# One core's bulk loads moved from SyncE's DMA queue to GpSimd's, with the large SBUF tensor at a multiple of 256 bytes

## The chip, the cores and the metric

The kernel runs on one core of a Trainium2 chip. The metric is the device time of one execution in microseconds (us). The time before is the median of 3 runs. A run and its profile are two things: the profile is one execution recorded by the hardware profiler, and its span runs from the first to the last instruction.

## The reference

One decode step of two branches that are mixed by a scalar gate: attention of one query against a cache of 65,536 keys and values in 32 heads, and a small gated feed-forward network. Everything is bfloat16.

```python
# x (1,1,512); k_cache, v_cache (1,32,65536,128); wq (512,4096); wo (4096,512)
# w_gate, w_up (512,1792); w_down (1792,512); gate_w (512)
g = sigmoid((x * gate_w).sum(-1))
q = (x @ wq)                                   # 32 heads of 128
scores = einsum(q, k_cache) * 128 ** -0.5      # 32 x 65536
p = softmax(scores)
a = einsum(p, v_cache) @ wo
b = (silu(x @ w_gate) * (x @ w_up)) @ w_down
return g * a + (1 - g) * b
```

The caches are 2 x 537 MB and each byte of them is used once, so nearly all of the 1,088 MB that the kernel reads are keys and values.

## The kernel before

A head's keys are 16.8 MB and are loaded in two halves, z = 0 and z = 1, of 8.4 MB; its values likewise. One such load is one DMA: 128 partitions, each a contiguous row of 64 KiB in HBM and in SBUF. All of them go into one large SBUF tensor, `mem` (128 partitions x 188,416 bytes), in which a place is counted in KiB: `KA`, `KZ` and `V0` are places for key halves, `VA` and `VZ` for value halves. The places overlap, so a load may start only when what lay there has been used.

What is done with a half: VectorE transposes keys in 8 pieces of 128 x 2048 four-byte words into `kt` (line 322 for head 0, lines 415 and 422 for later heads; each piece counts `ktdone` up by one), TensorE makes the scores from `kt` (line 472, `qkdone`), then the maximum, the exponential on ScalarE and a re-ordering of the probabilities on VectorE (line 331, 16 short copies for each half) follow, and TensorE multiplies the probabilities with the values straight from `mem` (line 525, 40 and 24 matmuls to a half, `pvdone`). A head's values are worked on while the next head's keys are being scored.

SyncE issues nearly all DMAs, in the order in which it is written, and waits ahead of each until the place is free. Its order: the four weights `wq`, `wg`, `wu`, `wd` (line 213); the first key half of head 0 as two DMAs of half the columns, `ka0` and `ka` (line 228); then, when the query is there (`s_q`), the second key half of head 0; when the 8 pieces of the first half are transposed (`ktdone` = 8), the first key half of head 1; when 13 are, the first value half of head 0; and so on. From head 1 the loop is key half 0 of the head after, value half 0, key half 1, value half 1, each behind one wait (lines 241 to 249):

```python
sp.wait_ge(s_q, 1)
load("k", 0, 1)
sp.wait_ge(ktdone, NP)          # NP = 8
load("k", 1, 0)
...
sp.wait_ge(pvdone, i * 4 + 7)
load("v", i + 1, 0)
```

The last value half is cut into 8 DMAs of falling size (line 258), and `wo` comes ahead of them, so that little work is left when the last bytes land. ScalarE issues the two 1 KB loads of `x` and `gate_w` at the start and half of the output; SyncE issues the other half of it. GpSimd has only four small memsets of constants at the start.

`mem` is allocated behind 16,384 bytes of reserved space and a few small constants, at byte 16,512 of each partition, which is 128 past a multiple of 256. All places in `mem` are multiples of 1,024 bytes from there.

Of the kernel before, what the change touches and what calls it, by code (L numbers as in the profile page):

```python
# [5 lines left out]
P = 128  # L6
KB = 512
# [5 lines left out]
BF16 = mybir.dt.bfloat16  # L13
# [8 lines left out]
def bass_gated_mix__mha_block_cached__swiglu_ffn__decode_kernel(  # L22
# [11 lines left out]
    out: bass.AP,  # L34
):
    _, H, S, Dh = A_k_cache.shape
    D = A_wq.shape[0]
    F = B_w_gate.shape[1]
# [3 lines left out]
    HR = R // 2  # L42
    NP = HR // PR
# [5 lines left out]
    KA, KZ, VA, VZ, V0 = 32, 0, 120, 96, 96  # L49
    MEM = 184  # L50
# [12 lines left out]
    WOJ, WO31 = V0, V0 + 1  # L63

    with ExitStack() as ctx:
        def sb(name, shape, dt):
            return ctx.enter_context(nc.sbuf_tensor(name, shape, dt))

        def psum(name, shape, dt):
            return ctx.enter_context(nc.psum_tensor(name, shape, dt))  # L70
# [1 line left out]
        def sem(name):  # L72
            return ctx.enter_context(nc.semaphore(name))
# [7 lines left out]
        psW = psum("psW", [P, 512], F32)  # L81
        psZ = psum("psZ", [P, 512], F32)

        mem = sb("mem", [P, MEM * KB], BF16)
        kt = sb("kt", [P, 2, 2 * PR * 32], U32)
        qd = sb("qd", [P, H, 4, 4], BF16)
        qcur = sb("qcur", [P, 4, 4], BF16)
        pa = sb("pa", [P, 512], BF16)
# [18 lines left out]
        fin = sb("fin", [P, 128], BF16)  # L107

        def at(kb, n):
            return mem[:, kb * KB:kb * KB + n]  # L110
# [7 lines left out]
        mrow, amx, Lt = psM[0:1, 0:128], psM[:, 256:257], psM[:, 257:258]  # L118
        gm = sc[0:1, 5:6]

        names = ("x", "gw", "wq", "wg", "wu", "wd", "ka0", "ka", "kz", "va", "vz", "wo", "wj", "w31")
        d = {n: sem("d_" + n) for n in names}
        dt_ = [sem(f"d_t{i}") for i in range(len(tail))]
        s_ones = sem("s_ones")
# [15 lines left out]
        s_q = sem("s_q")  # L140
# [7 lines left out]
        s_b = sem("s_b")  # L148
        s_dch = sem("s_dch")
        ktdone = sem("ktdone")  # L150
        qkdone = sem("qkdone")
        pvdone = sem("pvdone")
# [22 lines left out]
        s_fin = sem("s_fin")  # L175
        s_zz = sem("s_zz")
        s_out2 = sem("s_out2")
# [3 lines left out]
        out_dram = out.rearrange("a b (c n) -> (a b c) n", c=4)  # L181
        gw_dram = gate_w.rearrange("(a d) -> a d", a=1)
        w_dram = {
            "wq": A_wq.rearrange("(p c) n -> p (c n)", c=Dc),
            "wg": B_w_gate.rearrange("(p c) f -> p (c f)", c=Dc),
            "wu": B_w_up.rearrange("(p c) f -> p (c f)", c=Dc),
            "wd": B_w_down.rearrange("(p c) n -> p (c n)", c=FC),
            "wo": A_wo.rearrange("(p j) n -> p (j n)", p=P),
        }
        wj_dram = w_dram["wo"][:, 31 * D:32 * D]  # L190
        w31_dram = A_wo.rearrange("(h d) n -> h d n", d=Dh)[H - 1]
        WQ, WG, WU, WD, WO = V0, 0, 14, V0 + 64, 64
# [8 lines left out]
        def place(kind, h, z):  # L201
            if kind == "k":
                return (KA, V0)[z] if isinstance(h, int) and h == 0 else (KA, KZ)[z]
            return (VA, VZ)[z]

        def kv_dram(cache, h):
            if isinstance(h, int):
                return cache[0, h].rearrange("(b p r) d -> b p (r d)", b=2, p=P)
            return cache[0, ds(h, 1)].rearrange("a (b p r) d -> b (a p) (r d)", b=2, p=P)

        for n, kb in (("wq", WQ), ("wg", WG), ("wu", WU), ("wd", WD)):
            src = w_dram[n]
# [4 lines left out]
        ctx.callback(lambda: nc.sync.wait_ge(s_out2, 16))  # L217
        block = ctx.enter_context(nc.Block())

        @block.sync  # L220
        def _(sp):
            def load(kind, h, z):
                cache = A_k_cache if kind == "k" else A_v_cache
                sp.dma_start(at(place(kind, h, z), HR * Dh), kv_dram(cache, h)[z]).then_inc(d[kind + "az"[z]], 16)  # L224

            half = HR // 2 * Dh
            for n in range(2):
                sp.dma_start(at(KA + 32 * n, half), kv_dram(A_k_cache, 0)[0][:, n * half:n * half + half]).then_inc(
                    (d["ka0"], d["ka"])[n], 16)
            sp.wait_ge(s_q, 1)  # L230
            load("k", 0, 1)
            sp.wait_ge(ktdone, NP)
            load("k", 1, 0)
            sp.wait_ge(ktdone, 2 * NP - 3)
            sp.wait_ge(s_b, 1)
            load("v", 0, 0)
            sp.wait_ge(ktdone, 2 * NP + NP // 2)
            load("k", 1, 1)
            sp.wait_ge(pvdone, 5)
            load("v", 0, 1)  # L240
            with nc.sync.Fori(0, H - 2) as i:
                sp.wait_ge(ktdone, i * (2 * NP) + (4 * NP - 4))
                load("k", i + 2, 0)
                sp.wait_ge(pvdone, i * 4 + 7)
                load("v", i + 1, 0)
                sp.wait_ge(ktdone, i * (2 * NP) + (4 * NP + NP // 2))
                load("k", i + 2, 1)
                sp.wait_ge(pvdone, i * 4 + 9)
                load("v", i + 1, 1)
            sp.wait_ge(ktdone, 2 * NP * H - NP)  # L250
            sp.dma_start(at(WO, 31 * D), w_dram["wo"][:, 0:31 * D]).then_inc(d["wo"], 16)
            src = A_v_cache[0, H - 1].rearrange("(b p r) d -> b p (r d)", b=2, p=P)
            need = {0: (ktdone, 2 * NP * H - 4), 1: (ktdone, 2 * NP * H), 2: (pvdone, 4 * H - 1)}
            for n, (kb, r0, nr) in enumerate(tail):
                if n in need:
                    sp.wait_ge(*need[n])
                b, o = divmod(r0, HR)
                sp.dma_start(at(kb, nr * Dh), src[b][:, o * Dh:(o + nr) * Dh]).then_inc(dt_[n], 16)  # L258
            sp.wait_ge(pvdone, 4 * H)
            sp.dma_start(at(WOJ, D), wj_dram).then_inc(d["wj"], 16)  # L260
            sp.dma_start(at(WO31, D), w31_dram).then_inc(d["w31"], 16)
            sp.wait_ge(s_fin, 1)
            sp.dma_start(out_dram[2:4, :], fin[32:34, :]).then_inc(s_out2, 16)

        @block.scalar
        def _(act):
# [38 lines left out]
        def _(dve):  # L305
# [7 lines left out]
            def transposes(z):  # L313
                dve.wait_ge(d[("ka0", "kz")[z]], 16)
                for c, u in enumerate(k_order[z]):
                    i = NP * z + c
                    if i == NP // 2:
                        dve.wait_ge(d["ka"], 16)
                    if i >= 2:
                        dve.wait_ge(qkdone, i - 1)  # L320
                    src = at(place("k", 0, z) + 8 * u, PR * Dh).bitcast(U32)
                    nc.vector.transpose(kt[:, i % 2, :].rearrange("p (j r t) -> p r j t", j=2, t=32),  # L322
                                        src.rearrange("p (r j t) -> p r j t", j=2, t=32)).then_inc(ktdone, 1)

            def shuffle(z, s):
                c0 = 256 * z
                for g in range(4):
                    for b in range(4):
                        dst = pb[32 * g:32 * g + 32, c0:c0 + 256].rearrange("p (n b) -> p n b", b=4)[:, :, b]
                        sr = pa[32 * b:32 * b + 32, c0:c0 + 256].rearrange("p (n g) -> p n g", g=4)[:, :, g]  # L330
                        last = nc.vector.tensor_copy(dst, sr)  # L331
                last.then_inc(s, 1)
# [7 lines left out]
            def late(pv, sl, so):  # L340
                dve.wait_ge(pvdone, pv)
                shuffle(1, s_pbz)
                dve.wait_ge(s_L, sl)
                dve.wait_ge(s_or, so)
                nc.vector.reciprocal(Li, Lt).then_inc(s_li, 1)
# [57 lines left out]
            with nc.vector.Fori(1, H) as i:  # L403
                n = i * (2 * NP)
                v = i * 4
                dma = i * 16
                dve.wait_ge(d["ka"], dma + 16)
                for c, u in enumerate(k_order[0]):
                    if c == NP // 2:
                        dve.wait_ge(expdone, i)  # L410
                        dve.wait_ge(pvdone, v - 2)
                        shuffle(0, s_pba)
                    dve.wait_ge(qkdone, n + (c - 1))
                    src = at(KA + 8 * u, PR * Dh).bitcast(U32)
                    nc.vector.transpose(kt[:, c % 2, :].rearrange("p (j r t) -> p r j t", j=2, t=32),  # L415
                                        src.rearrange("p (r j t) -> p r j t", j=2, t=32)).then_inc(ktdone, 1)
                late(v, i, i)
                dve.wait_ge(d["kz"], dma + 16)
                for c, u in enumerate(k_order[1]):
                    dve.wait_ge(qkdone, n + (NP + c - 1))  # L420
                    src = at(KZ + 8 * u, PR * Dh).bitcast(U32)
                    nc.vector.transpose(kt[:, c % 2, :].rearrange("p (j r t) -> p r j t", j=2, t=32),  # L422
                                        src.rearrange("p (r j t) -> p r j t", j=2, t=32)).then_inc(ktdone, 1)
                top(i, n + 2 * NP)
# [206 lines left out]
```

## Time and profile before

| | |
|---|---|
| time, median of 3 runs | 2518.53 us (2518.48 to 2519.13) |
| profiled execution, first to last instruction (span) | 2517.0 us |
| busy: TensorE, VectorE, ScalarE, GpSimd | 68%, 56%, 3%, 0% |
| bytes read from HBM | 1087.77 MB, 432 GB/s over the span |
| SyncE's DMA queue (q1), share of the 16 DMA engines' span | 99.9% |

The profiled execution's own time is known only as its span. It is 1.5 us below the median of the runs, which also count what lies around the first and last instruction. In the views, "SPq" is SyncE's queue of instructions, "PEld" TensorE's weight load, and "to landing" the time from the issue of a DMA to its last semaphore increment. A wait is written as the engine and line that waited, and after an arrow what ended the wait.

### The profile page before, as it was taken

To read this page: it belongs to the slowest core of one execution; us is meant where nothing else is said; L and a number is where in the kernel's file an instruction comes from. 1 tells how busy PE (TensorE), PEld (TensorE's weight loads), DVE (VectorE), ACT (ScalarE), POOL (GpSimd) and SP (SyncE) were. 2 spreads that over 40 slices of the span, in tenths; PEclk is the share of its full clock that TensorE was granted. 3 is DMA by queue.
4 is the path that set the end of the run, shared out by engine and by line. 5 is a ranking of instruction groups with operands and counts; after the bars stand their busy time and mean duration, and the time that the engine had idled before them with its cause. 6 is when DMAs were issued, how large, how long until landed. Compare 5 with 4: busy or idle time off the path is not lost.

```text
span 2517.0 us, 51694 instructions
## 1 busy us (share of the span) xinstructions
PE 1710.9 (68%) x21624; PEld 979.2 (39%) x21624; DVE 1411.7 (56%) x1683; ACT 64.6 (3%) x195; POOL 0.2 (0%) x4
## 2 busy tenths in 40 slices
PE   4667756667667677676776766766767767667677
PEld 3334433333433334333443333343334433334334
DVE  4764565554655645646456555465564564645653
ACT  0000000000000000000000000000000000000000
POOL 0000000000000000000000000000000000000000
PEclk8577767677677676776776767767767767677677
DMA  9999999999999999999999999999999999999999
GB/s 419 435 433 433 433 433 433 433 434 433 434 433 433 433 433 433 433 433 433 433 433 433 433 433 434 435 433 434 434 433 433 434 434 433 433 433 433 434 433 395
DMA packets 20471, 1087.93 MB, mean 432 GB/s; under 512 B 2283, under 2 KB 2669, under 8 KB 2925
## 3 DMA queue, kind: packets, MB, share of 16 engines
q1 hardware_dynamic: 20452, 1087.78, 99.9%
q8 instruction: 9, 0.15, 0.0%
q14 instruction: 2, 0.01, 0.0%
q10 hardware_dynamic: 8, 0.00, 0.0%
HBM read 1087.77 MB, written 0.00 MB: 432 GB/s over the span
## 4 chain that ended last, share of the span: by engine, by line
DMA 71%; PE 27%; DVE 1%; issue 1%; SPq 0%; ACT 0%; DVEq 0%
DMA mem<-in_A_v_cache_dram 68%; PE psO L525 27%; DMA mem<-in_A_k_cache_dram 2%; DVE kt L322 1%; DMA mem<-in_A_wq_dram 0%; DVE kt L415 0%; SPq L224 0%; PE psM L456 0%; DVE pb L331 0%; PE psS L472 0%; SPq L258 0%; PE psZ L600 0%; DVE sm L336 0%; PE psW L561 0%; PE psM L547 0%
## 5 line engine op out<-in xcount | busy, mean ns | idle before, releaser
L472 PE MATMUL psS<-qcur,kt 128*128 128x4 bf16 x16384 | 573.0, 169 | 728.7 <-DVE kt L415 413.2
L525 PE MATMUL psO<-mem,pb 128*4 128x512 bf16 x3968 | 1042.3, 429 | 34.5 <-DMA mem<-in_A_v_cache_dram 34.1
L472 PEld LDWEIGHTS psS<-qcur,kt 128*128 128x128 bf16 x16384 | 534.0, 105 | 792.1 <-issue 789.7
L422 DVE STREAM_TRANSPOSE kt<-mem 128x2048 uint32<-128x2048 uint32 x248 | 547.6, 2275 | 405.9 <-DMA mem<-in_A_k_cache_dram 405.9
L415 DVE STREAM_TRANSPOSE kt<-mem 128x2048 uint32<-128x2048 uint32 x248 | 551.3, 2280 | 239.3 <-DMA mem<-in_A_k_cache_dram 238.3
L525 PEld LDWEIGHTS psO<-mem,pb 128*4 128x4 bf16 x3968 | 359.8, 93 | 660.4 <-issue 241.3
L331 DVE COPY pb<-pa 32x64 bf16<-32x64 bf16 x1024 | 233.5, 228 | 15.1 <-ACT pa L288 1.5
L338 DVE TENSOR_REDUCE sc<-psM 1x1 f32<-1x128 f32 x32 | 8.9, 279 | 334.9 <-PE psM L547 334.9
L336 DVE TENSOR_REDUCE sm<-psS 128x1 f32<-128x512 f32 x32 | 22.1, 692 | 42.2 <-PE psS L472 42.2
L322 DVE STREAM_TRANSPOSE kt<-mem 128x2048 uint32<-128x2048 uint32 x16 | 35.4, 2277 | 16.9 <-DMA mem<-in_A_k_cache_dram 16.9
L286 ACT ACTIVATE sm<-psM 128x1 f32<-128x1 f32 x32 | 5.5, 171 | 1223.4 <-PE psM L549 1223.4
L282 ACT ACTIVATE oTn<-psT,gcol 128x1 f32 (+1 forms) x31 | 8.2, 264 | 1036.8 <-PE psT L499 1036.8
L499 PE MATMUL psT<-ident,orow 4*128 4x1 f32 x256 | 33.5, 248 | 0.5 <-ACT orow L280 0.5
L499 PEld LDWEIGHTS psT<-ident,orow 4*128 4x128 f32 x256 | 30.8, 186 | 1.2 <-ACT orow L280 0.6
L280 ACT ACTIVATE orow<-psO,sm 4x512 f32<-4x512 f32 x31 | 21.0, 678 | 130.3 <-PE psO L525 126.0
L288 ACT ACTIVATE pa<-psS,sm 128x512 bf16<-128x512 f32 x32 | 22.0, 687 | 1.0
L549 PE MATMUL psM<-sc,onesf 1*128 1x1 f32 x64 | 12.3, 259 | 11.9 <-DVE sc L338 11.9
L561 PE MATMUL psW<-pb,mem 128*128 128x1 bf16 x512 | 14.6, 165 | 6.5 <-DMA mem<-in_A_v_cache_dram 6.0
L549 PEld LDWEIGHTS psM<-sc,onesf 1*128 1x128 f32 x64 | 9.6, 186 | 21.5 <-DVE sc L338 21.5
L561 PEld LDWEIGHTS psW<-pb,mem 128*128 128x128 bf16 x512 | 14.1, 102 | 7.6 <-issue 5.5
L553 PEld LDWEIGHTS psM<-sm,onesf 128*128 128x128 f32 x64 | 9.7, 191 | 14.7 <-issue 13.5
L553 PE MATMUL psM<-sm,onesf 128*128 128x1 f32 x64 | 12.4, 264 | 1.1 <-ACT pa L288 1.1
(72 smaller groups left out, 93.1 us busy)
## 6 DMA issues: line engine op xcount, KB each, us to landing
mem<-in_A_v_cache_dram SPq DMA_DIRECT2D x3, 4096.0 KB, 29.4
mem<-in_A_k_cache_dram SPq DMA_DIRECT2D x2, 4096.0 KB, 38.9
mem<-in_A_wq_dram SPq DMA_DIRECT2D x1, 4096.0 KB, 12.3
mem<-in_A_wo_dram SPq DMA_DIRECT2D x1, 3968.0 KB, 36.6
mem<-in_A_v_cache_dram SPq DMA_DIRECT2D x1, 2048.0 KB, 32.9
mem<-in_B_w_gate_dram SPq DMA_DIRECT2D x1, 1792.0 KB, 16.1
mem<-in_B_w_up_dram SPq DMA_DIRECT2D x1, 1792.0 KB, 21.4
mem<-in_B_w_down_dram SPq DMA_DIRECT2D x1, 1792.0 KB, 25.2
```

Source lines behind the costliest of these rows:

```text
L288: nc.scalar.activation(pa[:], psS[:], ACT.Exp, bias=nbias, scale=SCALE, accum_out=rsum).then_inc(expdone, 1)
L322: nc.vector.transpose(kt[:, i % 2, :].rearrange("p (j r t) -> p r j t", j=2, t=32), src.rearrange("p (r j t) -> p r j t", j=2, t=32)).then ...
L331: last = nc.vector.tensor_copy(dst, sr)
L336: nc.vector.reduce_max(mxs, psS[:], AX_X).then_inc(s_mx, 1)
L415: nc.vector.transpose(kt[:, c % 2, :].rearrange("p (j r t) -> p r j t", j=2, t=32), src.rearrange("p (r j t) -> p r j t", j=2, t=32)).then ...
L422: nc.vector.transpose(kt[:, c % 2, :].rearrange("p (j r t) -> p r j t", j=2, t=32), src.rearrange("p (r j t) -> p r j t", j=2, t=32)).then ...
L472: last = nc.tensor.matmul(psS[:, o:o + 4] if j is None else psS[:, ds(j * (2 * PR) + o, 4)], ktb[b][:, je // 2, r, :, je % 2], qcur[:, je, ...
L499: last = nc.tensor.matmul(psT[:, 0:1], orow[0:4, i * Dh:(i + 1) * Dh], ident[0:4, i:i + 1], start=(i == 0), stop=(i == 3))
L525: last = nc.tensor.matmul(psO[0:4, :], pb[:, k_col[256 * z + r]:k_col[256 * z + r] + 4], vt[:, r * Dh:(r + 4) * Dh], start=(z == 0 and par ...
L549: nc.tensor.matmul(amx, onesf[0:1, :], gm, start=True, stop=True).then_inc(s_ar, 1)
L553: nc.tensor.matmul(Lt, onesf[:], rsum, start=True, stop=True).then_inc(s_L, 1)
L561: last = nc.tensor.matmul(psW[:, 0:1], vt[:, r * Dh:(r + 1) * Dh], pb[:, col:col + 1], start=(r0 + r == 0), stop=(r0 + r == R - 1))
```

## The change

All DMAs behind `ka0` and `ka` are written in a program of GpSimd's, with the same waits in the same order; SyncE keeps the four weights, the first key half of head 0 and its half of the output. The second piece of that first key half has a semaphore of its own, `ka1`, since the later key halves count theirs from another queue. `mem` is placed at a multiple of 256 bytes: it moves from byte 16,512 to byte 16,640 of each partition. The instructions of TensorE, VectorE and ScalarE stay as they are and in their order; GpSimd gets 136 DMAs and their waits.

```diff
-        def sb(name, shape, dt):
-            return ctx.enter_context(nc.sbuf_tensor(name, shape, dt))
+        def sb(name, shape, dt, align=32):
+            return ctx.enter_context(nc.sbuf_tensor(name, shape, dt, align_bytes=align))
...
-        mem = sb("mem", [P, MEM * KB], BF16)
+        mem = sb("mem", [P, MEM * KB], BF16, 256)
...
         @block.sync
         def _(sp):
+            for n in range(2):
+                sp.dma_start(at(KA + 32 * n, half), kv_dram(A_k_cache, 0)[0][:, n * half:n * half + half]).then_inc(
+                    (d["ka0"], d["ka1"])[n], 16)
+            sp.wait_ge(s_fin, 1)
+            sp.dma_start(out_dram[2:4, :], fin[32:34, :]).then_inc(s_out2, 16)
+
+        @block.gpsimd
+        def _(pool):
             def load(kind, h, z):
                 cache = A_k_cache if kind == "k" else A_v_cache
-                sp.dma_start(at(place(kind, h, z), HR * Dh), kv_dram(cache, h)[z]).then_inc(d[kind + "az"[z]], 16)
-
-            half = HR // 2 * Dh
-            for n in range(2):
-                sp.dma_start(at(KA + 32 * n, half), kv_dram(A_k_cache, 0)[0][:, n * half:n * half + half]).then_inc(
-                    (d["ka0"], d["ka"])[n], 16)
-            sp.wait_ge(s_q, 1)
+                pool.dma_start(at(place(kind, h, z), HR * Dh), kv_dram(cache, h)[z]).then_inc(d[kind + "az"[z]], 16)
+
+            pool.wait_ge(s_q, 1)
             load("k", 0, 1)
-            sp.wait_ge(ktdone, NP)
+            pool.wait_ge(ktdone, NP)
             load("k", 1, 0)
...
-            with nc.sync.Fori(0, H - 2) as i:
-                sp.wait_ge(ktdone, i * (2 * NP) + (4 * NP - 4))
+            with nc.gpsimd.Fori(0, H - 2) as i:
+                pool.wait_ge(ktdone, i * (2 * NP) + (4 * NP - 4))
                 load("k", i + 2, 0)
...
                     if i == NP // 2:
-                        dve.wait_ge(d["ka"], 16)
+                        dve.wait_ge(d["ka1"], 16)
...
-                dve.wait_ge(d["ka"], dma + 16)
+                dve.wait_ge(d["ka"], dma)
```

More of the change, by code (lines that the diff above doesn't have):

```diff
@@ L119, in bass_gated_mix__mha_block_cached__swiglu_ffn__decode_kernel @@
         gm = sc[0:1, 5:6]
-        names = ("x", "gw", "wq", "wg", "wu", "wd", "ka0", "ka", "kz", "va", "vz", "wo", "wj", "w31")
+        names = ("x", "gw", "wq", "wg", "wu", "wd", "ka0", "ka1", "ka", "kz", "va", "vz", "wo", "wj", "w31")
         d = {n: sem("d_" + n) for n in names}
@@ L218, in bass_gated_mix__mha_block_cached__swiglu_ffn__decode_kernel @@
         block = ctx.enter_context(nc.Block())
+        half = HR // 2 * Dh
         @block.sync
         def _(sp):
+            for n in range(2):
[5 more added lines that the diff above has]
+        def _(pool):
             def load(kind, h, z):
@@ L231, in _ @@
+            pool.wait_ge(s_q, 1)
             load("k", 0, 1)
-            sp.wait_ge(ktdone, NP)
+            pool.wait_ge(ktdone, NP)
             load("k", 1, 0)
-            sp.wait_ge(ktdone, 2 * NP - 3)
-            sp.wait_ge(s_b, 1)
+            pool.wait_ge(ktdone, 2 * NP - 3)
+            pool.wait_ge(s_b, 1)
             load("v", 0, 0)
-            sp.wait_ge(ktdone, 2 * NP + NP // 2)
+            pool.wait_ge(ktdone, 2 * NP + NP // 2)
             load("k", 1, 1)
-            sp.wait_ge(pvdone, 5)
+            pool.wait_ge(pvdone, 5)
@@ L240, in _ @@
             load("v", 0, 1)
-            with nc.sync.Fori(0, H - 2) as i:
-                sp.wait_ge(ktdone, i * (2 * NP) + (4 * NP - 4))
+            with nc.gpsimd.Fori(0, H - 2) as i:
+                pool.wait_ge(ktdone, i * (2 * NP) + (4 * NP - 4))
                 load("k", i + 2, 0)
-                sp.wait_ge(pvdone, i * 4 + 7)
+                pool.wait_ge(pvdone, i * 4 + 7)
                 load("v", i + 1, 0)
-                sp.wait_ge(ktdone, i * (2 * NP) + (4 * NP + NP // 2))
+                pool.wait_ge(ktdone, i * (2 * NP) + (4 * NP + NP // 2))
@@ L247, in _ @@
                 load("k", i + 2, 1)
-                sp.wait_ge(pvdone, i * 4 + 9)
+                pool.wait_ge(pvdone, i * 4 + 9)
                 load("v", i + 1, 1)
-            sp.wait_ge(ktdone, 2 * NP * H - NP)
-            sp.dma_start(at(WO, 31 * D), w_dram["wo"][:, 0:31 * D]).then_inc(d["wo"], 16)
+            pool.wait_ge(ktdone, 2 * NP * H - NP)
+            pool.dma_start(at(WO, 31 * D), w_dram["wo"][:, 0:31 * D]).then_inc(d["wo"], 16)
             src = A_v_cache[0, H - 1].rearrange("(b p r) d -> b p (r d)", b=2, p=P)
@@ L255, in _ @@
                 if n in need:
-                    sp.wait_ge(*need[n])
+                    pool.wait_ge(*need[n])
                 b, o = divmod(r0, HR)
[L258 to L263, printed above, removed]
+                pool.dma_start(at(kb, nr * Dh), src[b][:, o * Dh:(o + nr) * Dh]).then_inc(dt_[n], 16)
+            pool.wait_ge(pvdone, 4 * H)
+            pool.dma_start(at(WOJ, D), wj_dram).then_inc(d["wj"], 16)
+            pool.dma_start(at(WO31, D), w31_dram).then_inc(d["w31"], 16)
         @block.scalar
```

## Prediction

> **What bounds the kernel now.** I read the profile page first, the part on DMA, because the kernel reads 1,088 MB and computes little on each byte.
>
> ```profile
> PE 1710.9 (68%) x21624; PEld 979.2 (39%) x21624; DVE 1411.7 (56%) x1683; ACT 64.6 (3%) x195; POOL 0.2 (0%) x4
> ...
> GB/s 419 435 433 433 433 433 433 433 434 433 434 433 433 433 433 433 433 433 433 433 433 433 433 433 434 435 433 434 434 433 433 434 434 433 433 433 433 434 433 395
> DMA packets 20471, 1087.93 MB, mean 432 GB/s; under 512 B 2283, under 2 KB 2669, under 8 KB 2925
> ...
> q1 hardware_dynamic: 20452, 1087.78, 99.9%
> ```
>
> No compute engine is busy over 68%, while the packets of SyncE's queue fill 99.9% of the 16 DMA engines' time. The rate is flat at 433 to 435 GB/s but for the first and last slices. Next, the table by stretches, to see whether any stage has free DMA time.
>
> ```profile
> 40.00:66.00 26.00, 8.69 (x247) 8.03 (x244) 14.88 (x7) 0.00 (x0) 0.00 (x0) 0.53 1.01 433
> 66.00:90.00 24.00, 11.65 (x278) 10.31 (x278) 21.77 (x12) 1.04 (x4) 0.00 (x0) 0.50 1.00 434
> ...
> 170.00:2470.00 2300.00, 1580.72 (x19500) 892.56 (x19499) 1304.42 (x1526) 57.80 (x175) 0.00 (x0) 0.72 1.00 433
> ```
>
> The last two columns are the DMA share and the rate. The share is 1.00 early as well as late, so the time is bytes over rate. Two things follow. A microsecond in which the DMA engines have nothing queued is never won back, and only a better rate shortens the kernel. Then the chain of waits, for what stands between two loads.
>
> ```profile
> 1122.87 26.89 DMA mem<-in_A_v_cache_dram
> 1149.81 11.04 PE psO L525 x40
> 1160.87 0.05 SPq L224
> 1161.02 27.44 DMA mem<-in_A_v_cache_dram
> 1188.50 10.48 PE psO L525 x40
> ```
>
> It alternates: a value half lands, TensorE uses 40 matmuls' worth of it, the next value half is issued. From 1149.81 to 1188.50 are 38.69 us, in which one key half and one value half arrive, so one half takes 19.35 us of transfer.
>
> **Issue by GpSimd in the steady part.** GpSimd's four memsets are its whole work, so the DMAs wait behind nothing there; its waits are SyncE's, in SyncE's order.
>
> ```profile
> L224 SPq DMA_DIRECT2D mem<-in_A_k_cache_dram x63: 327/333/343, 16.8 to 2416.7; - x63
> ...
> DMA to landing us min/median/max: 26.7/28.4/49.4
> ```
>
> These are line 224's loads (ns of issue, then us to landing). The shortest time to landing is 26.7 us against 19.35 us of transfer: at every issue at least 7.3 us of older data are still queued. A 1 KB load from ScalarE's queue took 1.4 us from issue (0.74) to the start of the matmul that reads it (2.14, below); that leaves 5.9 us of cover for whatever GpSimd takes longer than SyncE. No row shows GpSimd issuing a DMA. The nearest is SyncE's 0.33 us. I take 0 for the steady part, since it needs 18 times that to use up the cover. Beyond the cover each microsecond would be paid in each of 62 value loads.
>
> A second thing that could hold GpSimd up is VectorE.
>
> ```profile
> L415 DVE STREAM_TRANSPOSE kt<-mem 128x2048 uint32<-128x2048 uint32 x248 | 551.3, 2280 | 239.3 <-DMA mem<-in_A_k_cache_dram 238.3
> ...
> L331 DVE COPY pb<-pa 32x64 bf16<-32x64 bf16 x1024 | 233.5, 228 | 15.1 <-ACT pa L288 1.5
> ```
>
> One instruction lasts 2.28 us at most, the 16 copies of line 331 together 16 x 0.23 = 3.7 us, both less than 5.9 us, so even a full block is hidden in the steady part. The Trainium skill (SBUF — State Buffer, "Who interferes with whom") says that VectorE copies in a two-port mode lock GpSimd out of the port through which it writes descriptors, which speaks against this change; by it the sum would change by no more than one such block, 3.7 us, at the one issue without cover (below), and no row here shows it.
>
> **The start: two queues in place of one.** This is the part that the diff hides. In one queue the second key half of head 0, K(0,1), lay behind everything older.
>
> ```profile
> 0.74 0.54 ACTq L214 DMA_DIRECT2D mem<-in_A_x_dram  x1
> 0.74 0.41 SPq L213 DMA_DIRECT2D mem<-in_A_wq_dram  x1
> ...
> 1.32 0.22 ACTq L215 DMA_DIRECT2D mem<-in_gate_w_dram  x1
> ...
> 1.68 0.43 SPq L213 DMA_DIRECT2D mem<-in_B_w_up_dram  x1
> ...
> 2.14 0.26 PE L450 MATMUL psM<-ones,mem 1*128 1x1 bf16 x4 [2.14 <-DMA mem<-in_A_x_dram]
> 2.15 0.53 SPq L213 DMA_DIRECT2D mem<-in_B_w_down_dram  x1
> ...
> 8.00 0.68 DVE L377 CUSTOM_DVE_ANT_0 mem<-mem 1x512 f32<-1x512 bf16 x1
> ...
> 13.19 0.96 PE L456 MATMUL psM<-xTb,mem 128*128 128x1 bf16 x31 [10.79 <-DMA mem<-in_A_wq_dram]
> ```
>
> Line 377 reads `gate_w`, so that load, issued on ScalarE's queue at 1.32, had landed by 8.00. `wq`, issued earlier on SyncE's queue, landed only at 13.2. A DMA of another queue therefore doesn't wait for the older queue's data; the engines serve both. Now the start in the same view, later:
>
> ```profile
> 16.77 39.29 SPq L224 DMA_DIRECT2D mem<-in_A_k_cache_dram  x2
> ...
> 37.10 8.89 DVE L322 STREAM_TRANSPOSE kt<-mem 128x2048 uint32<-128x2048 uint32 x4 [5.65 <-DMA mem<-in_A_k_cache_dram]
> ...
> 46.82 8.89 DVE L322 STREAM_TRANSPOSE kt<-mem 128x2048 uint32<-128x2048 uint32 x4 [0.82 <-DMA mem<-in_A_k_cache_dram]
> ...
> 66.17 17.66 DVE L322 STREAM_TRANSPOSE kt<-mem 128x2048 uint32<-128x2048 uint32 x8 [10.46 <-DMA mem<-in_A_k_cache_dram]
> ```
>
> Before: `ka0` lands at 37.1, `ka` at 46.8, K(0,1), issued at 16.77, at 66.2. The eighth transpose ends at 46.82 + 8.89 = 55.7, the next half K(1,0) is issued then, 10 us before the queue would run dry.
>
> After: K(0,1) is issued at 16.8 on GpSimd's queue, with `wu`, `wd`, `ka0` and `ka1` still to come on SyncE's. If the engines alternate packet by packet, with one row of a load to a packet (128 rows over 16 engines, 8 to each), its 8 packets per engine pass after 8 of SyncE's, and SyncE's remaining data are pushed back by all 19.35 us of it. Then `ka1` is what lands last, at 46.8 + 19.35 = 66.2. Its four transposes take 8.89 us, so K(1,0) is issued at 75.1, and its first bytes come some 1.4 us later, at 76.5. From 66.2 to 76.5 the DMA engines have nothing: +10.3 us. GpSimd's longer issue is exposed just here, once: at least 0, at most one full block of 3.7 us; I take 0.5, nearer to the 0.33 us that an issue costs SyncE. Sum +10.8, between +9 and +14. Behind it each load keeps its cover: 13 pieces are transposed at 75.1 + 5 x 2.2 = 86, ahead of K(1,0)'s landing at 96, and value half 0 follows; the steady alternation is as before, 10.8 us later.
>
> **The 256-byte address.** It can only change what a row costs beyond its bytes. `wu` lands at 1.68 + 21.4, `wd` at 2.15 + 25.2:
>
> ```profile
> mem<-in_B_w_up_dram SPq DMA_DIRECT2D x1, 1792.0 KB, 21.4
> mem<-in_B_w_down_dram SPq DMA_DIRECT2D x1, 1792.0 KB, 25.2
> ```
>
> so 8 rows of 14 KB take 4.27 us, 534 ns a row, on each of 16 engines. From 37.10 to 46.82, 8 rows of 32 KB take 1215 ns each; 16 rows of 64 KB in 38.69 us take 2418 ns each. Twice 1215 less 2418 leaves 12 ns a row that don't scale with bytes; 534 less 14/64 of 2418 leaves 5 ns. There are (20471 - 2283) / 16 = 1137 rows to an engine, so the ends are 0 and -1137 x 12 ns = -13.6 us. The row price holds all that a row costs, its start, its end and its semaphores; the change moves only where its writing begins. I take a sixth, 2 ns a row, -2.3 us, nearer to nothing since no row of this trace shows an aligned load. The Trainium skill (DMA: Bandwidth & Descriptors, "How a descriptor splits into AXI transactions") says that a descriptor which does not start at a multiple of 256 bytes pays for the bytes below its start too; it tells this of reading, here the address written moves, and by it each row would save 128 bytes, as in the first rival.
>
> **Sum.** On the profiled span 2517.0: +10.8 - 2.3 = +8.5. The span lies 1.5 us under the median of the runs, which I leave as it is: 2518.5 + 8.5 = **2527.0 us**, with bounds of its own: +9 for the start and -4 for the address (short of the first rival's 5.3) give 2523.5, +14 and 0 give 2532.5.
>
> **The rivals.** *The address pays for 128 bytes a row.* A 64 KB row is written 128 bytes past the boundary; if those are 128 bytes of time, 128/65536 of 2418 ns is 4.7 ns a row, 1137 x 4.7 ns = -5.3 us instead of -2.3: 2524.0. It lies within the row price of 5 to 12 ns, which speaks for it; that bytes written need not be padded speaks against it. Above named page's rule gives this time.
>
> *GpSimd's queue doesn't overtake: faster or equal.* If fewer than half of K(0,1) (10.3 of its 19.35 us is the span in which the DMAs must still have work after `ka1` has landed) is served ahead of `ka1`, the gap is filled: K(1,0) is issued before the data run out. For instance, if the engines favour the queue that was first, or GpSimd's packets are much smaller than SyncE's. Then 2518.5 - 2.3 = 2516.2, with the 4.7 ns a row 2513.2. For it: `gate_w` took over 5 us to land. Against it: it landed before `wq`.
>
> *GpSimd's loads are dearer.* If it cuts each of the 1000 rows of 64 KB per engine (63 key and 62 value halves, 8 rows each) in two, 12 ns more for each is +12 us: 2539. If it needs 7 us longer to issue, the cover of 5.9 us is short by 1.1 us in 62 loads: +68 us. Against both: nothing in the trace, which has no GpSimd DMA; for them neither.
>
> **How the numbers follow.** Forecast 0.49, the address's 128 bytes with the gap 0.2, no overtaking 0.15, dearer loads 0.16. What a measurement of this kernel can tell from no change is about 0.2%, 5 us: faster is below 2513.5, slower above 2523.5. Faster: half of no overtaking, 0.08. Same: the other half, 0.07, and half of the 128 bytes, whose 2524.0 lies on the bound, 0.1: 0.17. Slower: the rest, 0.75. The range reaches down to 2515, where the whole row price of 13.6 us would be saved behind a gap of 10.8 (2515.7); it leaves out the fastest of no overtaking (0.07) and above 2535 most of the dearer loads (0.12). The forecast's own range is 2523.5 to 2532.5.
>
> **What would show it.** Right: in the new trace `ka1`'s transposes start near 66 us, after K(0,1) has long landed; the DMA share between 66 and 76 us is near 0 and the rate behind it 433 to 434 GB/s; GpSimd's issue row is under 6 us. Wrong: transposes of the fifth piece near 47 us or no hole in DMA; a steady period that differs from 38.69 us by over 0.1 us, which is 62 x 0.1 = 6 us in all; or holes between loads later on.

## The result and the profile after

The changed kernel took 2527.47 us (median of 5 runs, 2527.21 to 2528.12) against 2518.48 (5 runs, 2518.20 to 2519.13): ratio 1.0036, 95% interval 1.0026 to 1.0047. It is 9.0 us slower. Forecast were 2527.0, +8.5. The profiled execution has a span of 2526.7, 9.7 over the one before. The total came out as forecast; the two terms that make it up were each too small, and their errors nearly cancel, which is luck (below).

The page, the rows that answer to those shown of before:

```profile
PE 1708.3 (68%) x21624; PEld 978.0 (39%) x21624; DVE 1412.3 (56%) x1683; ACT 64.7 (3%) x195; POOL 73.3 (3%) x140
...
GB/s 419 348 433 431 433 433 432 432 444 434 433 433 432 432 441 437 432 434 432 432 440 438 432 433 433 432 432 442 436 433 433 432 432 441 437 432 434 432 432 402
...
q0 software_dynamic: 19232, 1069.69, 97.7%
q1 hardware_dynamic: 868, 18.09, 1.7%
```

The loads have moved to another queue, q0. The second slice of the rate, 63 to 126 us, has fallen from 435 to 348 GB/s; behind it each slice but the last holds 431 to 444. The table by stretches (the last two columns are DMA share and GB/s) and the start in order of time:

```profile
66.00:76.00 10.00, 4.79 (x143) 4.37 (x140) 10.00 (x5) 0.00 (x0) 0.54 (x1) 0.50 0.01 2
66.00:77.00 11.00, 4.79 (x143) 4.37 (x140) 11.00 (x6) 0.00 (x0) 0.54 (x1) 0.50 0.21 69
170.00:2470.00 2300.00, 1578.32 (x19492) 891.42 (x19491) 1307.77 (x1527) 58.49 (x176) 64.43 (x120) 0.72 1.00 434
```

```profile
17.13 0.67 POOL L234 DMA_DIRECT2D mem<-in_A_k_cache_dram  x1 [16.55 <-PE psM L460]
25.25 6.86 PE L488 MATMUL psM<-xTb,mem 128*128 128x1 bf16 x112 [7.34 <-DMA mem<-in_B_w_up_dram]
46.63 5.27 PE L496 MATMUL psY<-mem,guT 128*1 128x512 bf16 x14 [14.53 <-DMA mem<-in_B_w_down_dram]
56.27 8.89 DVE L326 STREAM_TRANSPOSE kt<-mem 128x2048 uint32<-128x2048 uint32 x4 [22.78 <-DMA mem<-in_A_k_cache_dram]
65.91 26.44 DVE L326 STREAM_TRANSPOSE kt<-mem 128x2048 uint32<-128x2048 uint32 x12 [0.76 <-DMA mem<-in_A_k_cache_dram]
75.12 0.54 POOL L234 DMA_DIRECT2D mem<-in_A_k_cache_dram  x1 [57.32 <-DVE kt L326]
98.14 8.89 DVE L419 STREAM_TRANSPOSE kt<-mem 128x2048 uint32<-128x2048 uint32 x4 [2.81 <-DMA mem<-in_A_k_cache_dram]
```

This is the forecast hole. `ka1`'s transposes start at 65.9 instead of 46.8, and no wait on K(0,1) parts the last twelve pieces: it had landed long before. The eighth piece ends at 74.8, GpSimd issues K(1,0) at 75.1, and from 66 to 76 us the DMA share is 0.01. (A packet is counted where it starts, so the 0.21 up to 77 us are the first packets of K(1,0).) `wd` landed at 46.6, 21.5 us behind `wu`, where one followed the other by 4.3 us; the 17.2 us more are about 7 packets of 2.42 us of K(0,1). That alone would look the same if K(0,1) had passed as one block. The packets that started from 25 to 36 us, about half of that stretch, show that the queues do take turns: 54 of K(0,1) (q0) and 62 of SyncE's (q1).

```profile
q0 software_dynamic: 54, 3.54, 74.5%
q1 hardware_dynamic: 62, 0.89, 18.8%
```

The chain of waits, the second value landing and the last one before the tail, before and then after:

```profile
143.60 10.69 PE psO L525 x40
...
2465.67 10.19 PE psO L525 x40
```

```profile
75.12 22.90 DMA mem<-in_A_k_cache_dram
...
156.31 10.67 PE psO L529 x40
...
2475.18 10.06 PE psO L529 x40
```

At the second landing the changed kernel is 12.7 us late, at the last 9.5. Between them lie 60 periods: 38.70 us each before, 38.65 after. So the start cost more than the end shows, and 3.2 us came back at a better rate.

### The profile page after: what moved, and what is told of

It reads as the page before. It is cut to its first block, busy times and chain, and to the rows that moved or that the text cites. A ratio compares the mean times of both kernels' runs of the same rounds, so it can differ in the third digit from the quotient of the medians.

```text
span 2526.7 us, 51725 instructions
## 1 busy us (share of the span) xinstructions
PE 1708.3 (68%) x21624; PEld 978.0 (39%) x21624; DVE 1412.3 (56%) x1683; ACT 64.7 (3%) x195; POOL 73.3 (3%) x140
## 4 chain that ended last, share of the span: by engine, by line
DMA 68%; PE 27%; issue 5%; POOLq 0%; DVE 0%; POOL 0%; ACT 0%; DVEq 0%
DMA mem<-in_A_v_cache_dram 67%; PE psO L529 26%; DMA mem<-in_A_k_cache_dram 1%; DMA mem<-in_A_wq_dram 0%; DVE kt L419 0%; POOLq L234 0%; PE psM L460 0%; POOL mem L264 0%; POOL mem L234 0%; PE psZ L604 0%; POOLq L247 0%; POOLq L252 0%; PE psW L565 0%; ACT fin L304 0%; DVEq L417 0%
## 5 line engine op out<-in xcount | busy, mean ns | idle before, releaser
L234 POOL DMA_DIRECT2D mem<-in_A_v_cache_dram x62 | 32.8, 529 | 1274.3 <-PE psO L529 1263.9
L234 POOL DMA_DIRECT2D mem<-in_A_k_cache_dram x63 | 34.4, 546 | 1106.2 <-DVE kt L419 525.0
L553 PE MATMUL psM<-sc,onesf 1*128 1x1 f32 x64 | 12.3, 259 | 11.9 <-DVE sc L342 11.9
L553 PEld LDWEIGHTS psM<-sc,onesf 1*128 1x128 f32 x64 | 9.6, 186 | 21.5 <-DVE sc L342 21.5
## 6 DMA issues: line engine op xcount, KB each, us to landing
mem<-in_A_wq_dram SPq DMA_DIRECT2D x1, 4096.0 KB, 12.3
mem<-in_B_w_down_dram SPq DMA_DIRECT2D x1, 1792.0 KB, 44.3
```

Source lines behind the costliest of these rows:

```text
L234: pool.dma_start(at(place(kind, h, z), HR * Dh), kv_dram(cache, h)[z]).then_inc(d[kind + "az"[z]], 16)
L553: nc.tensor.matmul(amx, onesf[0:1, :], gm, start=True, stop=True).then_inc(s_ar, 1)
```

## Experiments: the two parts by themselves

Theory: the loss is the hole at the start, made by a second queue, whoever issues on it; the better rate comes from the address. Rivals: the hole is GpSimd's lateness; the rate comes with GpSimd's queue.

**The address alone**, in the kernel before:

```diff
...
-        mem = sb("mem", [P, MEM * KB], BF16)
+        mem = sb("mem", [P, MEM * KB], BF16, 256)
```

> The kernel before with the large tensor at a multiple of 256 bytes and nothing else; all loads stay on SyncE. Between two value landings the changed kernel takes 38.64 us where the kernel before takes 38.69 to 38.70. Theory (the address saves 2.5 ns of each 64 KB row, the queue saves nothing): about 62 x 0.055 = 3.4 us less, 2515, and a period of 38.64 us. Rival (the lower period comes with GpSimd's queue): 2518.5, period 38.70. Rival (the address saves the time of 128 bytes in each row, 4.7 ns): 2513.2.

Measured: 2513.84 (11 runs, 2513.64 to 2514.52) against 2518.35; ratio 0.9982, interval 0.9973 to 0.9991. Its chain:

```profile
143.19 10.83 PE psO L525 x40
...
2461.44 10.54 PE psO L525 x40
```

60 periods of 38.64 us, without GpSimd: the rate is the address's. It saves 4.5 us, 4.0 ns on each of 1137 rows, twice the 2 ns taken in the prediction and nearer to the first rival's 4.7; the time, too, is nearer to the 2513.2 of that rival than to the expected 2515. This version is the fastest of the three, 0.18% below the kernel before.

**The queue alone**, in the changed kernel:

```diff
-        mem = sb("mem", [P, MEM * KB], BF16, 256)
+        mem = sb("mem", [P, MEM * KB], BF16)
```

> The changed kernel with the large tensor back at its old address, 128 bytes past a multiple of 256; GpSimd issues as in the changed kernel. Theory (gap at the start from the second queue, rate from the address): the gap stays and the period is 38.70 again: 2527.5 + 3.4 = 2531. Rival (the lower period comes with GpSimd's queue): 2527.5, period 38.64.

Measured: 2531.86 (2531.47 to 2532.13), ratio 1.0054, interval 1.0041 to 1.0068.

```profile
156.70 10.45 PE psO L529 x40
...
2478.76 11.62 PE psO L529 x40
```

Again 38.70 us a period: GpSimd's queue moves the steady loads at SyncE's rate. At the first of these landings as at the last it is 13.1 us behind the kernel before, so what the start lost stayed lost. The queue costs 13.5 us, the address gives 4.5 back, and 13.5 - 4.5 = 9.0 is the whole result.

**The same overtaking without GpSimd.** In the kernel before, ScalarE issues K(0,1), at the old address:

```diff
...
-            sp.wait_ge(s_q, 1)
-            load("k", 0, 1)
...
             nc.scalar.activation(sc[0:1, 1:2], sc[0:1, 0:1], ACT.Exp, scale=-1.0).then_inc(s_e1, 1)
+            act.wait_ge(s_q, 1)
+            act.dma_start(at(place("k", 0, 1), HR * Dh), kv_dram(A_k_cache, 0)[1]).then_inc(d["kz0"], 16)
...
```

> The kernel before, where only the second key half of head 0 is issued by ScalarE in place of SyncE, behind the same wait and with a semaphore of its own; old address, GpSimd issues nothing. Theory (any second queue lets that half overtake ka1): the hole at 66 us is there without GpSimd, and with the whole loss that the changed kernel has at its second value landing (12.7 us): 2531. Rival (the hole is GpSimd's): 2518.5.

Measured: 2531.15 (2531.04 to 2531.79), ratio 1.0051, interval 1.0038 to 1.0065. The start in order of time, and the stretch with the hole:

```profile
16.73 0.36 ACTq L268 DMA_DIRECT2D mem<-in_A_k_cache_dram  x1
...
66.16 26.44 DVE L322 STREAM_TRANSPOSE kt<-mem 128x2048 uint32<-128x2048 uint32 x12 [0.81 <-DMA mem<-in_A_k_cache_dram]
...
75.08 0.33 SPq L224 DMA_DIRECT2D mem<-in_A_k_cache_dram  x1
...
98.22 8.89 DVE L415 STREAM_TRANSPOSE kt<-mem 128x2048 uint32<-128x2048 uint32 x4 [2.63 <-DMA mem<-in_A_k_cache_dram]
```

```profile
66.00:77.00 11.00, 5.03 (x149) 4.61 (x146) 10.84 (x5) 0.00 (x0) 0.00 (x0) 0.50 0.29 98
```

One DMA moved to a second queue, no GpSimd in it, costs 12.8 of the 13.5 us. What GpSimd itself adds over the whole kernel is about 0.7 us, and the slowest of these runs (2531.79) lies above the fastest with GpSimd's queue (2531.47).

## Experiments: can GpSimd issue without the hole?

**K(0,1) back on SyncE, all later loads on GpSimd**, new address:

```diff
...
+            sp.wait_ge(s_q, 1)
+            sp.dma_start(at(place("k", 0, 1), HR * Dh), kv_dram(A_k_cache, 0)[1]).then_inc(d["kz0"], 16)
             sp.wait_ge(s_fin, 1)
...
-            pool.wait_ge(s_q, 1)
-            load("k", 0, 1)
...
```

> The changed kernel, but the second key half of head 0 is issued by SyncE behind the first half, with a semaphore of its own; all later loads by GpSimd, address at a multiple of 256. Theory (the 9 us are lost because that half overtakes ka1 and the data run out at 66 us): no hole at 66 us, ka1's transposes at 47 us again, 2518.5 - 3.4 = 2515. Rival (GpSimd's issue is late or dearer at every load): most of the loss stays, 2524 to 2527.

Measured: 2518.52 (11 runs, 2517.69 to 2520.55), ratio 1.0003, interval 0.9994 to 1.0012: neither 2515 nor 2524. The profile:

```profile
46.60 8.89 DVE L326 STREAM_TRANSPOSE kt<-mem 128x2048 uint32<-128x2048 uint32 x4 [0.77 <-DMA mem<-in_A_k_cache_dram]
55.80 0.67 POOL L236 DMA_DIRECT2D mem<-in_A_k_cache_dram  x1 [55.23 <-DVE kt L326]
73.13 17.66 DVE L326 STREAM_TRANSPOSE kt<-mem 128x2048 uint32<-128x2048 uint32 x8 [17.64 <-DMA mem<-in_A_k_cache_dram]
84.53 0.53 POOL L236 DMA_DIRECT2D mem<-in_A_v_cache_dram  x1 [28.05 <-DVE kt L326]
```

```profile
77.00:90.00 13.00, 7.02 (x192) 6.54 (x192) 13.00 (x7) 0.00 (x0) 0.53 (x1) 0.50 0.86 348
```

The first hole is gone, but the handover between the queues has only moved. GpSimd's first load is now K(1,0), issued at 55.8 while SyncE's K(0,1) is still coming in. The two share the engines, K(0,1) lands at 73.1 instead of 66.0, its transposes are late, the first value load behind them too, and the DMA share falls to 0.86 between 77 and 90. The expectation missed this because it reckoned with a hole at the old place only.

**A later handover**, the changed kernel with one wait more:

```diff
             pool.wait_ge(s_q, 1)
+            pool.wait_ge(ktdone, 3)
             load("k", 0, 1)
```

> The changed kernel with one wait more: GpSimd issues the second key half of head 0 only when 3 pieces of the first half are transposed (ktdone = 3, about 44 us) in place of at once behind s_q (17 us). All bulk loads behind the first half are GpSimd's, address at a multiple of 256. Theory (only the overtaking at the start costs): SyncE has about 1 us of ka1 left, so ka1 lands at 49 at the latest, no hole at 66 us; the time is that of the address alone, 2513.8, plus under 1 us for GpSimd's longer issue: 2514.5. Rival (GpSimd's loads cost more throughout): 2517 or more.

Measured: 2517.11 (11 runs, 2516.84 to 2517.42), ratio 0.9995, interval 0.9986 to 1.0004. And the same with `ktdone` = 1:

> As the run before, but behind 1 piece (ktdone = 1, about 39 us). Theory, by packets taken in turns: the half's first packets come at 41, when ka1 has 5.6 us or 4.6 rows to an engine left; each is pushed back by one 64 KB packet of 2.42 us, so ka1 lands at 57.7, its fourth transpose ends at 66.7, the data run out at 66.0, and the next load is a cold start: 2514.5 + 4.5 = 2519. Rival (the queue that is first keeps the engines until it is empty): 2514.5.

Measured: 2514.57 (11 runs, 2513.86 to 2517.58), ratio 0.9986, interval 0.9977 to 0.9995. The order was expected the other way round. First the run with 3 pieces:

```profile
44.35 0.67 POOL L234 DMA_DIRECT2D mem<-in_A_k_cache_dram  x1 [43.78 <-DVE kt L327]
46.66 8.89 DVE L327 STREAM_TRANSPOSE kt<-mem 128x2048 uint32<-128x2048 uint32 x4 [0.75 <-DMA mem<-in_A_k_cache_dram]
...
69.00 17.66 DVE L327 STREAM_TRANSPOSE kt<-mem 128x2048 uint32<-128x2048 uint32 x8 [13.45 <-DMA mem<-in_A_k_cache_dram]
```

```profile
44.00:48.00 4.00, 2.24 (x64) 2.06 (x62) 3.25 (x2) 0.00 (x0) 0.67 (x1) 0.50 0.85 279
```

The same stretch, and the landing of K(0,1), in the kernel with the address alone:

```profile
44.00:48.00 4.00, 2.03 (x60) 1.86 (x57) 3.22 (x2) 0.00 (x0) 0.00 (x0) 0.50 1.17 508
...
65.97 17.66 DVE L322 STREAM_TRANSPOSE kt<-mem 128x2048 uint32<-128x2048 uint32 x8 [10.60 <-DMA mem<-in_A_k_cache_dram]
```

And the run with 1 piece:

```profile
40.14 0.67 POOL L234 DMA_DIRECT2D mem<-in_A_k_cache_dram  x1 [39.57 <-DVE kt L327]
51.69 8.89 DVE L327 STREAM_TRANSPOSE kt<-mem 128x2048 uint32<-128x2048 uint32 x4 [5.59 <-DMA mem<-in_A_k_cache_dram]
60.89 0.54 POOL L234 DMA_DIRECT2D mem<-in_A_k_cache_dram  x1 [20.08 <-DVE kt L327]
66.17 17.66 DVE L327 STREAM_TRANSPOSE kt<-mem 128x2048 uint32<-128x2048 uint32 x8 [5.60 <-DMA mem<-in_A_k_cache_dram]
```

With 3 pieces the issue at 44.35 is too late: `ka1` has nearly gone, the DMA share from 44 to 48 is 0.85 against 1.17 with the address alone (over 1 because packets count where they start), and K(0,1) lands at 69.0, 3.0 us behind that kernel's 66.0; the time is 3.3 us behind it. The 2517.1 is the number of the rival, by which GpSimd's loads cost more throughout, but not for its reason: in the run with 1 piece the same loads are GpSimd's, and it took 2514.6.

With 1 piece, `ka1`'s transposes start at 51.7, not at the expected 57.7. The expectation put the half's first packets at 41, 0.9 us behind the issue. By the records of single packets in the trace they start at 44.3, 4.1 us behind it, when all but two of `ka1`'s 128 rows had begun. On the slowest engine the last row waited for one 64 KB packet and then the 4-byte packet that reports the landing (at 51.3) for another, so `ka1` was pushed back by about two packets of 2.42 us and not by 4.6. In the changed kernel it was the same: the first packets of K(0,1), issued at 17.1, start at 21.0. Why a new queue starts so late behind another queue's work, no run shows. So with the wait at the right place GpSimd's issue costs 0.7 us on the median over SyncE's (2514.57 against 2513.84, with single runs up to 2517.58), and its gain is nothing.

## Experiments: the address

All on SyncE's queue, with the large tensor moved by unused bytes ahead of it, or by a coarser alignment:

```diff
+        sb("pad", [P, 80], BF16)       # 32 past; [P, 48]: 224 past; [P, 96]: 64 past
         mem = sb("mem", [P, MEM * KB], BF16)
```

```diff
...
-        mem = sb("mem", [P, MEM * KB], BF16)
+        mem = sb("mem", [P, MEM * KB], BF16, 512)
```

> The kernel before with 160 unused bytes ahead of the large tensor, which then starts 32 bytes past a multiple of 256 (before: 128 past); all loads on SyncE. The kernel with a multiple of 256 took 2513.84, 4.5 us under the kernel before, or 4.0 ns in each of 1137 rows. Theory (a row pays for the bytes between the multiple of 256 below its start and its start): 32 bytes are 1.2 ns a row, 2513.84 + 1.3 = 2515.2. Rival (a row that crosses one 256-byte boundary more pays the same whatever the distance): 2518.4.

> As the run before, with 96 unused bytes, so that the tensor starts 224 bytes past a multiple of 256. Theory (a row pays for the bytes below its start): 224 bytes are 8.2 ns a row, 2513.84 + 9.4 = 2523.2. Rival (the same whatever the distance): 2518.4.

> The kernel before with the large tensor at a multiple of 512 bytes (byte 16,896; the multiple of 256 alone was byte 16,640), all loads on SyncE. Theory (256 is the whole step): 2513.8, as with the multiple of 256. Rival (each doubling of the alignment brings something, as 128 past took 1.2 us less than 32 or 224 past): about 2512.5.

> The kernel before with 192 unused bytes, so that the large tensor starts 64 bytes past a multiple of 256. Measured so far: 0 past 2513.8, 128 past 2518.5, 32 and 224 past 2519.7. Theory (any distance that is not a multiple of 128 costs the same): 2519.7. Rival (multiples of 64 are as 128 past): 2518.5. Rival (the cost grows with the distance): about 2516.

| start past a multiple of 256 | time, us | ratio to before, interval |
|---|---|---|
| 0 (multiple of 256) | 2513.84 | 0.9982 (0.9973 to 0.9991) |
| 0 (multiple of 512) | 2513.79 | 0.9982 (0.9973 to 0.9991) |
| 64 | 2518.83 | 1.0002 (0.9993 to 1.0011) |
| 128 (kernel before) | 2518.35 to 2518.48 | 1 |
| 32 | 2519.69 | 1.0005 (0.9996 to 1.0014) |
| 224 | 2519.73 | 1.0005 (0.9996 to 1.0014) |

The rate of the page, 32 past and then a multiple of 512:

```profile
GB/s 418 434 433 433 433 433 433 433 434 434 433 433 433 433 434 433 433 433 433 433 433 434 433 434 435 433 435 433 435 433 434 434 433 433 433 433 433 433 433 392
```

```profile
GB/s 419 434 434 435 434 434 434 434 434 434 435 434 435 435 434 434 434 434 434 434 434 434 434 434 434 434 434 434 434 434 434 435 434 435 435 435 434 434 435 399
```

One GB/s more in nearly every slice is the whole gain. The other tensors behind `mem` move with it, but the packets of the loads themselves are what gets shorter: from 200 to 2400 us a 64 KB packet lasts on average 2.4180 us at a multiple of 256, 2.4217 at 128 past, 2.4218 at 64 past and 2.4226 at 32 and at 224 past. The cost does not grow with the distance: 32 and 224 bytes past are equal, at 5.9 us or 5.1 ns a row, and 64 and 128 past cost 4.5 to 5.0 us. The expectations for 32 and 224 past, 2515.2 and 2523.2, are off by 4.5 and 3.5 us, on opposite sides; for 64 past the rival's 2518.5 came nearer than the expected 2519.7. So the rule that a row pays for the bytes below its start fails here, though at 128 past its price came near the measured one; the Trainium skill's account (DMA: Bandwidth & Descriptors, "How a descriptor splits into AXI transactions") tells it of reading, and these are writes. What fits is one boundary of 256 bytes more to each row at a nearly fixed price. Why 32 and 224 past cost 0.9 us more than 64 and 128 past is open; the intervals of their ratios overlap, though the packet lengths above stand in the same order.

## Why the prediction was right, step by step

- **What bounds it: right.** Lost DMA time was never won back: at the old address the 13.1 us of delay at the second value landing were still 13.1 at the last, and at the new one only the rate brought 3.2 of 12.7 us home.
- **The start: the mechanism right, the term too small.** `ka1` landing at 65.9 (66.2 forecast), the issue at 75.12 (75.1), the packets taking turns, all as worked out; the term was +10.8, measured 12.8 to 13.5 (bounds +9 to +14). What failed is the length of the hole, the step "From 66.2 to 76.5 the DMA engines have nothing: +10.3 us". From its issue to its first transpose K(1,0) took 23.0 us (75.12 to 98.14), 3.7 more than the 19.35 of transfer, where the sum had 1.4; issued by SyncE, behind ScalarE's overtaking, it took 23.1 (75.08 to 98.22). The packet records of the changed kernel show of what the 3.7 us consist. Averaged over the 16 engines, the first packets start 1.7 us behind the issue, they last 2.94 us instead of 2.42, and the last ones end 1.5 us ahead of the transposes. The 1.4 us were thus nearly right for the first bytes. Put at nothing were the longer first packets and that most engines run dry before a load is reported landed: `ka1`'s last packets ended at 64.2 on average, not at 66, so the engines were empty for 12.5 us and not for 10.3. The 1.4 us were read from a 1 KB load; the row of the same trace to take was `wq`, a large load on idle engines:

```profile
mem<-in_A_wq_dram SPq DMA_DIRECT2D x1, 4096.0 KB, 12.3
```

  12.3 us for what took 9.7 in the stream, so 2.6 and not 1.4 us for a load that finds the engines idle. With it the term is 12.0; the 3.7 of the 8.4 MB load, which no row of the trace before shows, brings it to 13.1.
- **Issue by GpSimd: right.** Its issue takes 0.53 us where SyncE took 0.33, and the cover hides it:

```profile
L234 POOL DMA_DIRECT2D mem<-in_A_v_cache_dram x62: 527/530/530, 86.1 to 2447.8; - x62
...
DMA to landing us min/median/max: 22.9/27.9/31.6
```

  The minimum is K(1,0) on the idle engines. It also shows that the cover was reckoned too large: of the 26.7 us that the shortest load of the kernel before took to land, 22.9 are what a load takes that finds nothing queued, so older data were 3.8 us of it and not 7.3. That is still far more than GpSimd's 0.2 us. (The 2.28 us called the most that a transpose lasts is their mean; the longest took 2.31.) By GpSimd at the old address,

```profile
75.38 0.54 POOL L234 DMA_DIRECT2D mem<-in_A_k_cache_dram  x1 [57.68 <-DVE kt L326]
...
98.73 8.89 DVE L419 STREAM_TRANSPOSE kt<-mem 128x2048 uint32<-128x2048 uint32 x4 [3.13 <-DMA mem<-in_A_k_cache_dram]
```

  it is 23.35 us from issue to the first transpose, by SyncE 23.14, and the whole time differed by 0.7 us; the 0.5 us taken for the one issue without cover lies between these 0.2 and 0.7. VectorE was transposing without a break at that moment and held GpSimd up by no more than that; the rule of the Trainium skill (SBUF — State Buffer, "Who interferes with whom") on copies in a two-port mode was not tried at that issue, since no copies ran then.
- **The address: direction right, size half.** -2.3 was taken, -4.5 measured, inside the 0 to -13.6 of the row price but past the -4 with which the forecast's range was drawn. The choice of a sixth of the row price had no row behind it; the rival's 128 bytes gave -5.3.
- **The sum** was right to 0.5 us because the start was 2.7 us too small and the address 2.2 us too small. That they cancel is luck. The range of 2523.5 to 2532.5 would have held the time had only one of them been off (2529.7 or 2524.8).
- **The rivals.** "Doesn't overtake" fell with `wd` at 46.6; "dearer loads" with 38.70 us a period at the old address.

## What to carry to other kernels

When DMAs are moved to another engine, write down for each moved one what it used to stand behind: the order within a queue is a dependency that no semaphore states, and a later load that is served alongside an earlier one delays the work that issues the next. In a kernel whose DMA engines never rest, price each place where the queue could run dry as the time from the last landing to the next issue, plus what a large load that finds the engines idle takes beyond its transfer. And put a tensor that receives large loads at a multiple of 256 bytes: 0.18% for one argument here.

## What was not expected of the hardware

- A load's row that starts off a multiple of 256 bytes in SBUF costs 4.0 to 5.1 ns more, at any of the four distances tried (32, 64, 128, 224), out of 2418 ns for 64 KB.
- An 8.4 MB load that starts on idle DMA engines is first used 3.7 to 4.0 us later than its transfer takes, on GpSimd's queue and on SyncE's; for 4.2 MB it was 2.6 us to the landing.
- A queue that joins while the engines are busy with another one starts late: its first packet came 3.9 us behind GpSimd's issue at 17.1, 3.6 behind ScalarE's at 16.7 and 4.1 behind GpSimd's at 40.1, but 1.2 behind the one at 75.1 on idle engines.
- The 4-byte packet that reports a landing takes its turn behind the other queue's packets like a row: 2.42 us of `ka1`'s delay with 1 piece.
- A handover between two queues is hit or missed by a few microseconds: 40.1 us gave 2514.6 with single runs up to 2517.6, 44.4 us gave 2517.1.
